# Runs of four up and four down products from place 32 on, a paired softmax, fewer filler products and a later clearing in a windowed attention with a feed-forward layer

## The chip, the cores and the metric

The kernel runs on one core of one Trainium2 chip. A core has five engines that work side by side and meet at semaphores: TensorE (PE, with its weight loads as PEld), VectorE (DVE), ScalarE (ACT), GpSimd (POOL) and SyncE (SP), which issues the DMAs. TensorE writes to PSUM, which has eight banks. The metric is the device time of one execution in microseconds (us).

## The reference

Attention in windows, and behind it a feed-forward layer whose weights are in two projections with a leaky bend between them:

```python
# q, k, v: (4, 8, 768, 64); mem_k, mem_v: (4, 8, 8, 64)
for c in range(nc):                       # chunks of 32 queries
    l_start = max(0, c_start - 16)
    r_end = min(S, c_end + 8)
    k_full = np.concatenate([mem_k, k[:, :, l_start:r_end]], axis=2)
    v_full = np.concatenate([mem_v, v[:, :, l_start:r_end]], axis=2)
    scores = scale * np.matmul(q_c, k_full.transpose(0, 1, 3, 2))
    scores = scores - np.max(scores, axis=-1, keepdims=True)
    a = np.exp(scores)
    a = a / (np.sum(a, axis=-1, keepdims=True) + 1e-09)
    out[:, :, c_start:c_end] = np.matmul(a, v_full)
...
# x: (3072, 512) from the attention; w_in: (512, 2048); w_out: (2048, 512)
h = x @ w_in
g = np.maximum(h, 0.0) + alpha * np.minimum(h, 0.0)
return (g @ w_out).astype(np.float32)
```

The two weights are float64 in memory. The kernel turns them into pairs of numbers (high and low) on the chip.

## The kernel before

**Tiles.** The 3072 tokens are 8 blocks of 384 (`NBLK`, `BT`). A block's attention is four units, one for each pair of heads (`NPAIR`), and leaves four tiles of x, each as a high and a low part (`xh`, `xl`). The 2048 inner columns are 16 tiles (`NF`). For a block and an f, `hidden` makes one *place*: an **up product** (L614: 12 matmuls of 384 columns into one of two PSUM banks, `h_ps`), then the bend (`below` on ACT, L623; `bend` on DVE, L626), the split of its result into `gh` and `gl` (L632, L636), and a **down product** (L644: 9 matmuls of 512 columns, added up in three banks, `o_ps`, over a block's f). There are 128 places. `ORDER` puts (0, f) and (1, f) side by side for the first nine f, so that places 0 to 17 use each weight twice while it is decoded; then blocks 0 and 1 finish, and from place 32 on each block's 16 places follow each other. The first two up products of a block are given out in four pieces of three matmuls, one for each x tile.

**Attention of the first two blocks** (units 0 to 7, `windows`). A unit is loaded as `early` (queries and keys in one DMA, values in another, L424; four buffers, so unit u + 4 waits for unit u). `score_products` (L271) writes one of the two banks `s_ps`; `top` (L439, L441, L443) hides what lies outside and takes the maximum, `less` (L447) subtracts it, `exps` (L451) is on ACT, `total` and `inverse` (L455, L458) give the divisor; GpSimd multiplies (L468, L472); `turn` (L480) transposes on TensorE into `o_ps` banks; ACT copies (L485); `values` (L493) makes the attention's output and `split` (L408, L412) the x parts. In front of each score product and each `turn`, `stir` (L257) issues some bfloat16 matmuls on a constant tile, whose output nobody reads: 8 before the first score product, 2 before each other, 1 before each `turn` (`STIR`).

**Attention of the later blocks.** `attend` gives TensorE a step with the values of one unit (L375) and the scores of the next (L289). The softmax (`scores`: L299 to L320), the weights (L334 to L344) and 14 transposes on DVE (L361) run beside the feed-forward. The transposes write only part of `pt`, and a copy only part of `e2`; the rest is cleared once by `zero` (L517, L520) on GpSimd, emitted after the eighth unit. `BEGIN` and `LATER` give the place at which a unit's scores are due; its weights are due three places later and its values four.

**Weights.** `load_w` loads each f's two tiles of 512 KB (L533); `decode` makes the pairs: `rebias` (ACT, L556), `gather` (L564), `ends` (DVE, L568), `join` (DVE, L572), `high` (ACT, L580), `low` (DVE, L583). The first two f are decoded tile by tile, w_in and w_out apart.

**What sets the order.** Every step is added to `Plan` with an engine, a cost in us, what it reads and writes, and often a due time `rest(place) = (128 - place) x PAIR`, PAIR being 4.7. `send` walks through time by these costs: the engine that can start first takes, of the steps that are ready by then, the one with the most time *behind* it. That is the larger of its own `rest` and of its cost, a hop and what its users have behind them:

```python
behind[n] = max(rest, cost + max((behind[m] + lag[engine] for m in users[n]), default=0.0))
```

Here `lag` is 0.07 (2.3 for a load). The order found is fixed in the program: each engine runs its queue in that order and waits at semaphores. An up product has `rest(place)`, a down product `rest(place + 1.5)`. The bends carry their up product's due time; `high` and `low` have none of their own. In a block's last place `store` copies the three `o_ps` banks with ACT (L691) and sends them out (L695); the next block's first down product needs these banks.

Of the kernel before, what the change touches and what calls it, by code (L numbers as in the profile page):

```python
# [89 lines left out]
STARTS_WIN = (0, 2 * LEFT, NKT - KW)  # L90
# [66 lines left out]
def body(ctx: ExitStack, tc: tile.TileContext, qvw, kw, first, w_in, w_out, alpha, out):  # L157
# [34 lines left out]

    es = [at.tile([P, NJ * 2, KW + 1], F32, name="e", tag=f"e{i}") for i in range(2)]
    for e in es:
        nc.gpsimd.memset(e[:, :, KW:], 1e-9)
    for ew in ews:
# [61 lines left out]

    def score_products(u):
        blk, pr = divmod(u, NPAIR)  # L260
        st = state[u]
        s_ps = ps_s.tile([P, 512], F32, name="s_ps", tag=f"s{u % 2}")
        stir(s_ps, STIR[0] if u == 0 else STIR[1])
        st["s"] = s_ps[:, :2 * NJ * KW].rearrange("p (n k) -> p n k", k=KW)
        t = early[u % NSET]
        q = t[:, :NQ].rearrange("p (c x) -> p c x", c=NT * NJ)
        keys = t[:, NQ:NQ + NT * NKT].rearrange("p (t k) -> p t k", t=NT)
        for n in range(2 * NJ):
            for i in range(2):
                t, j = n // NJ * 2 + i, n % NJ  # L270
                nc.tensor.matmul(  # L271
                    out=st["s"][i * 2 * CH:(i + 1) * 2 * CH, n],
                    lhsT=q[:, t * NJ + j],
                    rhs=keys[:, t, STARTS_WIN[j]:STARTS_WIN[j] + KW],
                    start=True, stop=True,
                )

    def head_products(u):

        st = state[u]  # L280
        st["s"] = [ps_s.tile([P, 512], F32, name="s_ps", tag=f"s{h2}")[:, :NJ * KW].rearrange("p (n k) -> p n k", n=NJ)
                   for h2 in range(2)]
# [20 lines left out]
    def scores(u):  # L303
# [11 lines left out]
        def exps(i):  # L315
            if i == 0:
                st["e"] = at.tile([P, NJ * 2, KW], F32, name="e", tag=f"e{u % 2}")
                st["den"] = sm.tile([P, NJ * 2, 1], F32, name="den", tag=f"den{u % 3}")
            n, h2 = divmod(i, 2)
            nc.scalar.activation(out=st["e"][:, i], in_=st["s"][h2][:, n], func=AF.Exp, scale=SCALE,  # L320
                                 bias=st["mx"][:, n, h2:h2 + 1], accum_out=st["den"][:, i])
# [4 lines left out]
        for i in range(NJ * 2):  # L326
            step(ACT, 0.54, partial(exps, i), reads=[("s", i % 2), ("mx", u % 3)],
                 writes=[("e", u % 2, i), ("den", u % 3, i)] if i else e_keys(u) + den_keys(u), rest=due(u))

# [89 lines left out]
    def load_first(u):  # L419
# [8 lines left out]
        step(SP, 0.78, partial(load, NQ + NT * NKT, NQ + NT * NKT + NV), writes=[("fv", u % NSET)], rest=due(u))  # L428

    def windows(u):  # L430

        st = state[u]
        sk, tks, ak = ("s", u % 2), [("o", 0), ("o", 1)], ("o", 2) if u % 2 else "a"
        ek = [("ew", u % NPT)]

        def top():
            s = st["s"]
            if u // NPAIR % 2 == 0:
                nc.vector.memset(s[0:2 * CH, 0, 0:LEFT], NEG)  # L439
            else:  # L440
                nc.vector.memset(s[2 * CH:4 * CH, 2 * NJ - 1, KW - NM - RIGHT:KW - NM], NEG)  # L441
            st["mx"] = sm.tile([P, NJ * 2, 1], F32, name="mx", tag=f"mx{u % 3}")
            nc.vector.tensor_reduce(out=st["mx"], in_=s, axis=AX.X, op=ALU.max)  # L443

        def less():
            st["e"] = es[u % 2][:, :, :KW]
            nc.vector.tensor_tensor(out=st["e"], in0=st["s"], in1=st["mx"].broadcast_to([P, NJ * 2, KW]),  # L447
                                    op=ALU.subtract)

        def exps():  # L450
            nc.scalar.activation(out=st["e"], in_=st["e"], func=AF.Exp, scale=SCALE)  # L451

        def total():
            st["den"] = sm.tile([P, NJ * 2, 1], F32, name="den", tag=f"den{u % 3}")
            nc.vector.tensor_reduce(out=st["den"], in_=es[u % 2], axis=AX.X, op=ALU.add)  # L455

        def inverse():
            nc.vector.reciprocal(out=st["den"], in_=st["den"])  # L458

# [39 lines left out]

        step(PE, 1.2, partial(score_products, u), reads=[("qk", u % NSET)], writes=[sk], rest=due(u))  # L500
        step(DVE, 0.66, top, writes=[sk, ("mx", u % 3)])
        step(DVE, 0.55, less, reads=[sk, ("mx", u % 3)], writes=e_keys(u))
        step(ACT, 0.52, exps, writes=e_keys(u))
        step(DVE, 0.56, total, reads=e_keys(u), writes=den_keys(u))
        step(DVE, 0.19, inverse, writes=den_keys(u))
        step(POOL, 0.62, partial(scale, 0), reads=den_keys(u) + e_keys(u), writes=ek)
        step(POOL, 0.5, partial(scale, 1), reads=den_keys(u) + e_keys(u), writes=ek)
        step(PE, 0.90, turn, reads=ek + ["eye"], writes=tks, rest=due(u, 1))
        for t in range(2):
# [37 lines left out]
    def decode_part(k, parts):  # L547
# [39 lines left out]
        if n == 1:  # L587
            step(*((ACT, 1.37) if k[1] else (DVE, 0.72)), partial(gather, [nc.scalar.copy if k[1] else nc.vector.tensor_copy]),
                 writes=r)
        elif f in GATHER_ACT:  # L590
            step(DVE, 0.72, partial(gather, [nc.vector.tensor_copy, None]), writes=r[:1])
            step(ACT, 1.37, partial(gather, [None, nc.scalar.copy]), writes=r[1:])
        else:
# [5 lines left out]
             writes=[("w", i, f, 1) for i in parts])  # L599

    def hidden(blk, f, first_f, last_f):

        first = blk * NPAIR
        joint = blk == 1 and f < NJOINT
        place = PLACE[blk, f]
        hk, sd, gh, gl = (x + str(place % 2) for x in ("h", "sd", "gh", "gl"))
        h = {}

        def up(ks):
            if ks[0] == 0:  # L610
                h["ps"] = ps_h.tile([P, 512], F32, name="h_ps", tag=hk)
            for k in ks:
# [16 lines left out]
        def high():  # L629
            h["gh"] = gp.tile([P, BT], F32R, name="gh", tag=gh)  # L630
            copy = nc.scalar.copy if place < HIGH_ACT else nc.vector.tensor_copy
            copy(out=h["gh"], in_=h["g"])  # L632

        def low():
            h["gl"] = gp.tile([P, BT], F32R, name="gl", tag=gl)
            nc.vector.tensor_tensor(out=h["gl"], in0=h["g"], in1=h["gh"].bitcast(F32), op=ALU.subtract)  # L636

        def down(o_ps):
            if f == first_f:
                banks = [(ps_o, f"o{i}") for i in range(NTT)] if not joint else [(ps_s, "s0"), (ps_s, "s1"), (ps_a, "a")]  # L640
                o_ps.extend(pool.tile([P, DM], F32, name="o_ps", tag=tag) for pool, tag in banks)
            for tt in range(NTT):
# [10 lines left out]
        def add_up():  # L653
            for ks in [[k] for k in range(NK)] if f < 2 else [list(range(NK))]:
                step(PE, 0.521 * len(ks), partial(up, ks),
                     reads=[("w", 0, f, 0), ("w", 0, f, 1)] + [(x, x_slot + k) for k in ks for x in ("xh", "xl")],
                     writes=[hk], rest=rest(place))

        def add_bend():
            step(ACT, 0.5, below, reads=[hk], writes=[sd], rest=rest(place))  # L660
            step(DVE, 0.62, bend, reads=["rise", hk], writes=[sd], rest=rest(place))
            step(*((ACT, 0.51) if place < HIGH_ACT else (DVE, 0.35)), high, reads=[sd], writes=[gh])
# [43 lines left out]
    def unit_begins(u):  # L706
        if u < NWIN:
            windows(u)
        else:
            scores(u)  # L710
# [113 lines left out]
```

## Time and profile before

| | us |
|---|---|
| median of 3 runs | 613.23 |
| lowest, highest | 612.78, 613.33 |
| the profiled execution, by its device time | 612.68 |
| its span, from the first to the last instruction | 610.9 |

The page gives the busy time of each engine and its share of the span, then the chain of work that ended last, followed back from the end. PE and PEld are one engine, so their times overlap. A matmul's own duration holds its way through the array; what a product costs is seen from the starts of the pieces in the chain. The rows by stretches of time give, after the stretch and its length, the busy time of PE, PEld, DVE, ACT and POOL, each with its count of instructions, then the granted TensorE clock, the share of DMA and GB/s. The first stretch of interest ends at about 33 us: until then the first eight units' attention, the loads and the first decoding run at once. Places 0 to 31 follow, until 171 us, then the blocks 2 to 7.

### The profile page before, as it was taken

To read this page: it belongs to the slowest core of one execution; us is meant where nothing else is said; L and a number is where in the kernel's file an instruction comes from. 1 tells how busy PE (TensorE), PEld (TensorE's weight loads), DVE (VectorE), ACT (ScalarE), POOL (GpSimd) and SP (SyncE) were. 2 spreads that over 40 slices of the span, in tenths; PEclk is the share of its full clock that TensorE was granted. 3 is DMA by queue.
4 is the path that set the end of the run, shared out by engine and by line. 5 is a ranking of instruction groups with operands and counts; after the bars stand their busy time and mean duration, and the time that the engine had idled before them with its cause. 6 is when DMAs were issued, how large, how long until landed. Compare 5 with 4: busy or idle time off the path is not lost.

```text
span 610.9 us, 11593 instructions
## 1 busy us (share of the span) xinstructions
PE 605.0 (99%) x4622; PEld 532.9 (87%) x4622; DVE 404.5 (66%) x1012; ACT 215.6 (35%) x596; POOL 34.6 (6%) x61
## 2 busy tenths in 40 slices
PE   8999999999999999999999999999999999999997
PEld 5789999889898888989889889888889888989986
DVE  5888999886777656666666666666666656633332
ACT  3788787634223222322223122322123222121111
POOL 3500000000000000000000000000000000000000
PEclk9999999999999999999999999999999999999999
DMA  8999400114121111201113101221002100010001
GB/s 340 352 408 410 164 0 1 33 32 150 25 96 49 50 50 49 99 3 50 49 50 101 42 9 49 84 67 50 20 30 101 50 18 19 0 54 1 0 1 52
DMA packets 20934, 48.99 MB, mean 80 GB/s; under 512 B 2448, under 2 KB 5520, under 8 KB 20880
## 3 DMA queue, kind: packets, MB, share of 16 engines
q1 hardware_dynamic: 20880, 48.25, 22.3%
q8 instruction: 36, 0.59, 0.4%
q14 instruction: 18, 0.15, 0.1%
HBM read 41.95 MB, written 6.29 MB: 79 GB/s over the span
## 4 chain that ended last, share of the span: by engine, by line
PE 97%; DVE 1%; DMA 1%; issue 0%; ACT 0%; SPq 0%; ACTq 0%
PE h_ps L614 44%; PE o_ps L644 44%; PE a_ps L375 3%; PE s_ps L289 3%; PE s_ps L257 1%; PE s_ps L271 1%; DMA w_t<-w_in 1%; PE a_ps L493 1%; PE o_ps L480 0%; DVE w_t L568 0%; PE o_ps L257 0%; DVE mx L443 0%; DVE e L447 0%; DVE w_t L564 0%; DVE xl L412 0%
## 5 line engine op out<-in xcount | busy, mean ns | idle before, releaser
L614 PE MATMUL h_ps<-xh,w 128*128 128x384 f32 x1024 | 261.6, 336 | 0.0
L644 PE MATMUL o_ps<-w,gh 128*128 128x512 f32 x768 | 240.7, 395 | 0.0
L614 PEld LDWEIGHTS h_ps<-xh,w 128*128 128x128 f32 x1024 | 185.7, 188 | 4.2
L614 PE MATMUL h_ps<-xl,w 128*128 128x384 f32 x512 | 174.6, 341 | 0.1
L644 PEld LDWEIGHTS o_ps<-w,gh 128*128 128x128 f32 x768 | 144.0, 188 | 27.8
L644 PE MATMUL o_ps<-w,gl 128*128 128x512 f32 x384 | 150.1, 391 | 0.0
L623 ACT ACTIVATE g<-h_ps 128x384 f32<-128x384 f32 x128 | 63.4, 496 | 245.2 <-PE h_ps L614 236.0
L626 DVE SCALAR_TENSOR_TENSOR g<-g,rise,h_ps 128x384 f32<-128x384 f32 x128 | 78.3, 612 | 94.4 <-ACT g L623 93.3
L361 DVE STREAM_TRANSPOSE pt<-e 32x192 f32<-32x192 f32 (+1 forms) x336 | 99.3, 300 | 11.1 <-POOL e L340 5.9
L614 PEld LDWEIGHTS h_ps<-xl,w 128*128 128x128 f32 x512 | 96.2, 188 | 6.5 <-DVE xl L412 0.3
L644 PEld LDWEIGHTS o_ps<-w,gl 128*128 128x128 f32 x384 | 72.1, 188 | 12.5
L636 DVE TENSOR_TENSOR gl<-g,gh 128x384 fp32r<-128x384 f32 x128 | 71.1, 557 | 4.6 <-ACT gh L632 1.4
L632 DVE CAST gh<-g 128x384 fp32r<-128x384 f32 x104 | 37.2, 360 | 54.2 <-PE o_ps L644 52.4
L320 ACT ACTIVATE e<-s_ps,mx 128x64 f32<-128x64 f32 x144 | 43.3, 320 | 39.7 <-DVE mx L313 39.7
L340 POOL TENSOR_TENSOR e<-e,den 128x384 f32<-128x384 f32 x24 | 20.1, 839 | 467.1 <-DVE den L337 457.4
L408 ACT CAST xh<-a_ps 128x384 fp32r<-128x384 f32 x32 | 15.4, 480 | 55.4 <-PE a_ps L375 53.6
L320 ACT ACTIVATION_READ_ACCUMULATOR e<-s_ps,mx 128x1 f32 x144 | 30.5, 212 | 0.0
L375 PEld LDWEIGHTS a_ps<-pt,v_t 128*64 128x64 f32 x384 | 16.6, 136 | 8.5 <-issue 8.5
L375 PE MATMUL a_ps<-pt,v_t 128*64 128x96 f32 x384 | 21.1, 252 | 0.0
L583 DVE TENSOR_TENSOR w<-a,w 128x1024 fp32r<-128x1024 f32 (+1 forms) x18 | 20.3, 1135 | 0.0
L572 DVE SCALAR_TENSOR_TENSOR a<-a,w_t 128x1024 int32<-128x1024 int32 (+1 forms) x18 | 19.8, 1102 | 0.2
L556 ACT ACTIVATE a<-w_t 128x1024 f32<-128x1024 f32 (+1 forms) x18 | 18.8, 1048 | 2.9 <-DMA w_t<-w_in 1.6
(52 smaller groups left out, 278.3 us busy)
## 6 DMA issues: line engine op xcount, KB each, us to landing
w_t<-w_in SPq DMA_DIRECT2D x16, 512.0 KB, 10.2
w_t<-w_out SPq DMA_DIRECT2D x16, 512.0 KB, 10.2
qk<-kw SPq DMA_DIRECT2D x24, 272.0 KB, 3.7
v_t<-qvw SPq DMA_DIRECT2D x24, 256.0 KB, 2.8
out<-o_t SPq DMA_DIRECT2D x24, 256.0 KB, 2.1
early<-first SPq DMA_DIRECT2D x8, 656.0 KB, 5.9
qk<-qvw SPq DMA_DIRECT2D x24, 192.0 KB, 3.6
early<-first SPq DMA_DIRECT2D x8, 256.0 KB, 5.9
```

What stands on the lines that cost most here:

```text
L320: nc.scalar.activation(out=st["e"][:, i], in_=st["s"][h2][:, n], func=AF.Exp, scale=SCALE, bias=st["mx"][:, n, h2:h2 + 1], accum_out=st["d ...
L340: nc.gpsimd.tensor_tensor(out=st["e"], in0=st["e"], in1=st["den"].broadcast_to([P, NJ * 2, KW]), op=ALU.mult)
L361: nc.vector.transpose(out=pts[u % NPT][quad * CH:(quad + 1) * CH, j, t0:t0 + n1 - n0].rearrange("p t h q -> p (t h) q"), in_=(st["e"], zer ...
L375: nc.tensor.matmul(out=st["a"][h2 * D:(h2 + 1) * D, t * TQ:(t + 1) * TQ], lhsT=st["v"][:, t, h2, :], rhs=pts[u % NPT][:, :, t, h2, :], sta ...
L572: nc.vector.scalar_tensor_tensor(out=d["a"], in0=d["a"], scalar=3, in1=d["t"][:, :, :, 1], op0=ALU.logical_shift_left, op1=ALU.bitwise_or)
L583: nc.vector.tensor_tensor(out=d["w"][:, :, 1], in0=d["a"].bitcast(F32), in1=d["w"][:, :, 0].bitcast(F32), op=ALU.subtract)
L614: nc.tensor.matmul(out=h["ps"][:, :BT], lhsT=ws[f, 0][:, wk, k * P:(k + 1) * P], rhs=xs[first + k][xk], start=(k == 0 and n == 0), stop=(k ...
L623: nc.scalar.activation(out=h["g"], in_=h["ps"][:, :BT], func=AF.Relu, scale=-1.0)
L626: nc.vector.scalar_tensor_tensor(out=h["g"], in0=h["g"], scalar=rise[:, f:f + 1], in1=h["ps"][:, :BT], op0=ALU.mult, op1=ALU.add)
L632: copy(out=h["gh"], in_=h["g"])
L636: nc.vector.tensor_tensor(out=h["gl"], in0=h["g"], in1=h["gh"].bitcast(F32), op=ALU.subtract)
L644: nc.tensor.matmul(out=o_ps[tt], lhsT=h[gk][:, tt * P:(tt + 1) * P], rhs=ws[f, 1][:, wk], start=(f == first_f and i == 0), stop=(f == last ...
```

## The change

Five things are changed.

- **Order.** From place 32 (`FIRST_RUN`) on, places are taken in groups of four (`RUN`). `up_at` and `down_at` replace the places in the due times. There are four `gh`/`gl` pairs instead of two (`NSUM`); the two new ones lie in the decode's tiles (`room`), and their first writers wait for the decode's last use of these.
- **Paired softmax.** Among the first eight units, 2 and 3, 4 and 5, and 6 and 7 go through `softmax` two at a time (`GROUPS`): one `tensor_reduce`, one subtraction, one exponential, one sum and one reciprocal for both. Units 4 and 5 have their scores in the two `h_ps` banks, which are now one tile, as the two `s_ps` banks are.
- **Fewer unread products.** `STIR` goes from (8, 2, 1) to (8, 0, 0), with the planned costs of the score product and of `turn` lowered to 0.76 and 0.68.
- **Later clearing.** `zero` is added when f reaches 9 in block 0, place 18, and waits for the decode of f = 8.
- **Due places.** `BEGIN` moves one place later, `LATER` two places earlier. The gather of the first w_out tile goes from ACT to DVE.

```diff
-BEGIN = {2: (3, 5, 7, 9)}
-LATER = (-1, 3, 7, 11)
-STIR = (8, 2, 1)
+BEGIN = {2: (4, 6, 8, 10)}
+NSUM = 4
+RUN, FIRST_RUN = 4, 32
+LATER = (-3, 1, 5, 9)
+STIR = (8, 0, 0)
+GROUPS = ((0,), (1,), (2, 3), (4, 5), (6, 7))
...
+    h_banks = ps_h.tile([P, 2, 512], F32, name="h_ps")
+    s_banks = ps_s.tile([P, 2, 512], F32, name="s_ps")
...
+    def softmax(us):
+        u0, n = us[0], len(us)
...
+        two, keys = (h_banks, ["h0", "h1"]) if u0 == 4 and n == 2 else (s_banks, [("s", 0), ("s", 1)])
+        here, ring = slice(u0 % 2, u0 % 2 + n), u0 // 2 % 2
...
+        view = two[:, here, :2 * NJ * KW].rearrange("p b (n k) -> p b n k", k=KW)
...
+            nc.vector.tensor_reduce(out=d["mx"], in_=view, axis=AX.X, op=ALU.max)
...
+            nc.vector.tensor_tensor(out=e[..., :KW], in0=view, in1=d["mx"].broadcast_to([P, n, NJ * 2, KW]),
+                                    op=ALU.subtract)
...
+            nc.scalar.activation(out=e[..., :KW], in_=e[..., :KW], func=AF.Exp, scale=SCALE)
...
+            nc.vector.tensor_reduce(out=d["den"], in_=e, axis=AX.X, op=ALU.add)
...
+            nc.vector.reciprocal(out=d["den"], in_=d["den"])
...
-            step(*((ACT, 1.37) if k[1] else (DVE, 0.72)), partial(gather, [nc.scalar.copy if k[1] else nc.vector.tensor_copy]),
-                 writes=r)
+            copy = nc.scalar.copy if k == (1, 1) else nc.vector.tensor_copy
+            step(*((ACT, 1.37) if k == (1, 1) else (DVE, 0.72)), partial(gather, [copy]), writes=r)
...
+    def room(name, tag):
+        n = int(tag[2:])
+        if n < 2:
+            return gp.tile([P, BT], F32R, name=name, tag=tag)
+        if name not in spare:
+            spare[name] = dec.tile([P, 2, DM], F32R, name=name, tag=f"a{len(spare)}")
+        return spare[name][:, n - 2, :BT]
...
+        up_at, down_at = place, place + 1.5
+        if place >= FIRST_RUN:
+            n = place % RUN
+            up_at = place - n + 0.58 + 0.5 * n
+            down_at = place - n + 0.5 * (RUN + n + 1) if n < RUN - 1 else place - n + 1.5 * RUN
...
-                     writes=[hk], rest=rest(place))
+                     writes=[hk], rest=rest(up_at))
...
-                 rest=rest(place + 1.5))
+                 rest=rest(down_at))
...
-    step(POOL, 3.0, zero, writes=["e2"] + [("pt", i, j) for i in range(NPT) for j in range(len(TURNS))] + [("ew", i) for i in range(NPT)])
...
+        if (blk, f) == (0, NJOINT):
+            step(POOL, 3.0, zero, reads=[("w", 1, f - 1, 1)], writes=["e2"] + [("ew", i) for i in range(NPT)]
+                 + [("pt", i, j) for i in range(NPT) for j in range(len(TURNS))])
```

More of the change, by code (lines that the diff above doesn't have):

```diff
@@ L191, in body @@
                             channel_multiplier=1)
-    es = [at.tile([P, NJ * 2, KW + 1], F32, name="e", tag=f"e{i}") for i in range(2)]
+    es = [at.tile([P, 2, NJ * 2, KW + 1], F32, name="e", tag=f"ee{i}") for i in range(2)]
     for e in es:
-        nc.gpsimd.memset(e[:, :, KW:], 1e-9)
+        nc.gpsimd.memset(e[..., KW:], 1e-9)
     for ew in ews:
@@ L257, in stir, with score_products @@
             nc.tensor.matmul(out=t, lhsT=busy[:, :P], rhs=busy, start=True, stop=True)
[L259 to L260 removed]
+    def score_products(u, bank):
         st = state[u]
[L262 to L264 removed]
+        stir(bank, STIR[0] if u == 0 else STIR[1])
+        s = bank[:, :2 * NJ * KW].rearrange("p (n k) -> p n k", k=KW)
         t = early[u % NSET]
@@ L280, in head_products @@
         st = state[u]
-        st["s"] = [ps_s.tile([P, 512], F32, name="s_ps", tag=f"s{h2}")[:, :NJ * KW].rearrange("p (n k) -> p n k", n=NJ)
-                   for h2 in range(2)]
+        st["s"] = [s_banks[:, h2, :NJ * KW].rearrange("p (n k) -> p n k", n=NJ) for h2 in range(2)]
         for n in range(NJ):
@@ L327, in scores @@
             step(ACT, 0.54, partial(exps, i), reads=[("s", i % 2), ("mx", u % 3)],
-                 writes=[("e", u % 2, i), ("den", u % 3, i)] if i else e_keys(u) + den_keys(u), rest=due(u))
+                 writes=[("e", u % 2, i), ("den", u % 3, i)] if i
+                 else e_keys(u) + den_keys(u) + [("ee", u % 2, j) for j in range(2)], rest=due(u))
     def weights(u):
@@ L428, in load_first, with top, less, exps @@
         step(SP, 0.78, partial(load, NQ + NT * NKT, NQ + NT * NKT + NV), writes=[("fv", u % NSET)], rest=due(u))
+    def softmax(us):
+        u0, n = us[0], len(us)
+        d = {}
+        two, keys = (h_banks, ["h0", "h1"]) if u0 == 4 and n == 2 else (s_banks, [("s", 0), ("s", 1)])
+        here, ring = slice(u0 % 2, u0 % 2 + n), u0 // 2 % 2
+        keys, e = keys[here], es[ring][:, here]
+        mk = [("mw", u0)]
+        dk, ek = [[(x, ring, i) for i in range(2)][here] for x in ("dw", "ee")]
+        view = two[:, here, :2 * NJ * KW].rearrange("p b (n k) -> p b n k", k=KW)
+        def top():
+            for i, u in enumerate(us):
+                if u // NPAIR % 2 == 0:
+                    nc.vector.memset(view[0:2 * CH, i, 0, 0:LEFT], NEG)
+                else:
+                    nc.vector.memset(view[2 * CH:4 * CH, i, 2 * NJ - 1, KW - NM - RIGHT:KW - NM], NEG)
+            d["mx"] = sm.tile([P, n, NJ * 2, 1], F32, name="mx", tag=f"mw{n}")
+            nc.vector.tensor_reduce(out=d["mx"], in_=view, axis=AX.X, op=ALU.max)
+        def less():
+            nc.vector.tensor_tensor(out=e[..., :KW], in0=view, in1=d["mx"].broadcast_to([P, n, NJ * 2, KW]),
+                                    op=ALU.subtract)
+        def exps():
+            nc.scalar.activation(out=e[..., :KW], in_=e[..., :KW], func=AF.Exp, scale=SCALE)
+        def total():
+            d["den"] = sm.tile([P, n, NJ * 2, 1], F32, name="den", tag=f"dw{n}{ring}")
+            nc.vector.tensor_reduce(out=d["den"], in_=e, axis=AX.X, op=ALU.add)
+        def inverse():
+            nc.vector.reciprocal(out=d["den"], in_=d["den"])
+            for i, u in enumerate(us):
+                state[u]["e"], state[u]["den"] = e[:, i, :, :KW], d["den"][:, i]
+        for u, key in zip(us, keys):
+            step(PE, 0.76, partial(score_products, u, two[:, u % 2]), reads=[("qk", u % NSET)], writes=[key], rest=due(u))
+        step(DVE, 0.13 + 0.04 + 0.4 * n + 0.065 * n, top, writes=keys + mk)
+        step(DVE, 0.14 + 0.4 * n, less, reads=keys + mk, writes=ek)
+        step(ACT, 0.2 + 0.32 * n, exps, writes=ek)
+        step(DVE, 0.15 + 0.41 * n, total, reads=ek, writes=dk)
+        step(DVE, 0.18 + 0.01 * n, inverse, writes=dk)
@@ L445, in less @@
[L445 to L455, printed above, removed]
@@ L498, in values @@
                     )
[L500 to L508, printed above, removed]
+        step(POOL, 0.62, partial(scale, 0), reads=dk + eu, writes=ek)
+        step(POOL, 0.5, partial(scale, 1), reads=dk + eu, writes=ek)
+        step(PE, 0.68, turn, reads=ek + ["eye"], writes=tks, rest=due(u, 1))
         for t in range(2):
@@ L605, in hidden @@
         place = PLACE[blk, f]
-        hk, sd, gh, gl = (x + str(place % 2) for x in ("h", "sd", "gh", "gl"))
+        hk, sd, gh, gl = (x + str(place % n)
+                          for x, n in (("h", 2), ("sd", 2), ("gh", NSUM), ("gl", NSUM)))
+        if place < FIRST_RUN:
+            gh, gl = f"gh{place % 2}", f"gl{place % 2}"
+        new = [("a", 0), ("a", 1)] if gh in ("gh2", "gh3") and place < FIRST_RUN + NSUM else []
+        up_at, down_at = place, place + 1.5
[3 more added lines that the diff above has]
+            down_at = place - n + 0.5 * (RUN + n + 1) if n < RUN - 1 else place - n + 1.5 * RUN
         h = {}
@@ L610, in up @@
             if ks[0] == 0:
-                h["ps"] = ps_h.tile([P, 512], F32, name="h_ps", tag=hk)
+                h["ps"] = h_banks[:, place % 2]
             for k in ks:
@@ L639, in down @@
             if f == first_f:
-                banks = [(ps_o, f"o{i}") for i in range(NTT)] if not joint else [(ps_s, "s0"), (ps_s, "s1"), (ps_a, "a")]
-                o_ps.extend(pool.tile([P, DM], F32, name="o_ps", tag=tag) for pool, tag in banks)
+                if joint:
+                    o_ps.extend([s_banks[:, 0], s_banks[:, 1], ps_a.tile([P, DM], F32, name="o_ps", tag="a")])
+                else:
+                    o_ps.extend(ps_o.tile([P, DM], F32, name="o_ps", tag=f"o{i}") for i in range(NTT))
             for tt in range(NTT):
@@ L656, in add_up @@
                      reads=[("w", 0, f, 0), ("w", 0, f, 1)] + [(x, x_slot + k) for k in ks for x in ("xh", "xl")],
-                     writes=[hk], rest=rest(place))
+                     writes=[hk], rest=rest(up_at))
         def add_bend():
-            step(ACT, 0.5, below, reads=[hk], writes=[sd], rest=rest(place))
-            step(DVE, 0.62, bend, reads=["rise", hk], writes=[sd], rest=rest(place))
-            step(*((ACT, 0.51) if place < HIGH_ACT else (DVE, 0.35)), high, reads=[sd], writes=[gh])
+            step(ACT, 0.5, below, reads=[hk], writes=[sd], rest=rest(up_at))
+            step(DVE, 0.62, bend, reads=["rise", hk], writes=[sd], rest=rest(up_at))
+            step(*((ACT, 0.51) if place < HIGH_ACT else (DVE, 0.35)), high, reads=[sd], writes=[gh] + new)
             step(DVE, 0.56, low, reads=[sd, gh], writes=[gl])
@@ L707, in unit_begins @@
         if u < NWIN:
+            for us in GROUPS:
+                if us[0] == u:
+                    softmax(us)
             windows(u)
```

23 lines of the change are left out of this document (7 added, 16 removed).

## The prediction

> **What bounds the kernel now.** I read the page first (busy time, then the chain of work that ended last), then the busy time by stretches, then the chain and the timeline in two places: the start and a steady piece.
>
> ```profile
> span 610.9 us, 11593 instructions
> ...
> PE 605.0 (99%) x4622; PEld 532.9 (87%) x4622; DVE 404.5 (66%) x1012; ACT 215.6 (35%) x596; POOL 34.6 (6%) x61
> ...
> PE 97%; DVE 1%; DMA 1%; issue 0%; ACT 0%; SPq 0%; ACTq 0%
> ```
>
> ```profile
> 5.00:24.00 19.00, 18.36 (x288) 13.20 (x288) 14.91 (x39) 9.10 (x20) 7.39 (x18) 1.00 0.99 376
> 24.00:33.50 9.50, 9.40 (x104) 7.55 (x102) 8.59 (x20) 8.45 (x19) 4.92 (x9) 1.00 1.00 375
> 33.50:45.00 11.50, 11.46 (x70) 10.31 (x71) 9.65 (x15) 9.43 (x15) 0.00 (x0) 1.00 1.02 411
> ...
> 300.00:611.00 311.00, 307.24 (x2219) 273.35 (x2217) 178.92 (x483) 74.14 (x253) 10.19 (x13) 1.00 0.12 39
> ```
>
> TensorE is the bound: 97% of the chain is PE. In the rows by stretches (time, length, then busy PE, PEld, DVE, ACT, POOL, clock, DMA share, GB/s) PE is busy throughout from 33.5 us, and in the last one its 3.8 us of idleness are the final copies and stores. So after 33.5 us a gain must make PE's own work shorter. Before that PE is busy too, but not all with work that anyone reads, and DMA (0.99, 1.00) and DVE (8.59 of 9.5 us) are close behind. These two stages are priced apart.
>
> **The steady stage: runs of four.** The chain in order of time (start us, us, what), pieces from four places:
>
> ```profile
> 51.02 4.12 PE o_ps L644 x18
> 55.14 4.18 PE h_ps L614 x24
> ...
> 82.34 2.10 PE h_ps L614 x12
> 84.45 2.08 PE o_ps L644 x9
> ...
> 171.34 1.06 PE h_ps L614 x6
> 172.40 2.08 PE o_ps L644 x9
> 174.48 5.22 PE h_ps L614 x30
> ...
> 601.08 6.18 PE o_ps L644 x27
> ```
>
> An up product is 12 matmuls, a down product 9. An up behind a down takes 2.10 us (82.34), a down behind an up 2.08 (84.45). But two downs in a row take 4.12, so the second costs 2.04: 0.04 less. Two ups in a row take 4.18, the second 2.08: 0.02 less; the 30 at 174.48 agree, as the 18 matmuls behind the first 12 take 3.12, and so do the 27 of the last downs, whose 6.18 holds PE's last drain. Each change of kind costs about 0.04 us into downs and 0.02 into ups, and the later product had its own waits as well, so it is the change of kind, not the start of a step.
>
> Place 32 begins at 171 us. From there to the end the timeline has 89 downs directly behind an up and 71 ups directly behind a down (first 172.40, last 601.08; the other runs start behind attention products).
>
> Which order does the new priority give? The planner takes, of the ready steps, the one with the most time behind it. An up carries its own cost, that of `below` and two hops, 2.72 us by the planner's numbers in the kernel, above its due time; that is 0.58 of PAIR. With `up_at` = group + 0.58 + 0.5n the ups rank at 0, 0.5, 1, 1.5; the downs at 2.5, 3, 3.5, and the fourth at 6, which is 2.0 in the next group. So a group reads: up 0, attention, up 1, up 2, up 3, the fourth down of the group before, then three downs. That is one change each way per group: 24 in 96 places. At the five block ends between places 48 and 112 the next block's first down must wait for the copies out of its banks, and I expect the planner to slip one up between: 29 each way. The attention products stand inside the ups now; their number stays, and their entry and exit are taken as equally dear, so they drop out. The sum: (89-29) x 0.04 + (71-29) x 0.02 = 2.4 + 0.8 = **3.2 us saved**.
>
> What hid the bends and may not now: `h_ps` has two banks, so up 2 waits for the bend of up 0, and up 3 for that of up 1. Before, a down stood between. At block starts three ups already run together:
>
> ```profile
> 385.62 0.36 DVE L310 TENSOR_REDUCE mx<-s_ps 128x3 f32<-128x192 f32 x1
> 385.90 0.55 DVE L412 TENSOR_TENSOR xl<-a_ps,xh 128x384 fp32r<-128x384 f32 x1
> ...
> 389.33 0.34 ACT L320 ACTIVATE e<-s_ps,mx 128x64 f32<-128x64 f32 x1
> 389.53 0.23 ACT L320 ACTIVATION_READ_ACCUMULATOR e<-s_ps,mx 128x1 f32 x1
> ...
> 395.92 0.33 PE L614 MATMUL h_ps<-xl,w 128*128 128x384 f32 x1
> ...
> 396.12 0.49 ACT L623 ACTIVATE g<-h_ps 128x384 f32<-128x384 f32 x1 [1.17 <-PE h_ps L614]
> ...
> 396.64 0.61 DVE L626 SCALAR_TENSOR_TENSOR g<-g,rise,h_ps 128x384 f32<-128x384 f32 x1 [0.43 <-ACT g L623]
> ...
> 398.00 0.33 PE L614 MATMUL h_ps<-xl,w 128*128 128x384 f32 x1
> ```
>
> The middle up starts at 395.92, `below` of the first at 396.12, its bend ends at 397.25, and the third up starts at 398.00: 0.75 us to spare. ACT's exponentials (0.43 us from one's start to its readout's end) and one DVE piece (0.55) can each stand in front, for the attention now falls into the up run: at worst 0.98 against 0.75, so 0.23 us per such up. The bounds are 0 and 24 x 2 x 0.23 = 11 us; the row nearest is the block start, where it is nothing, and both delays rarely meet, so I take 0.4 us. If ups 2 and 3 stall, PE idles, since the fourth down ranks behind up 3. `high` and `low` are covered by the later ups. The two further `gh`/`gl` pairs are needed for this: four downs wait with their inputs in store; they lie in the decode's tiles, free long before place 34.
>
> **The start.** The chain there, and five rows of its timeline:
>
> ```profile
> 1.45 3.60 PE s_ps L257 x8
> 5.05 1.48 PE s_ps L271 x24
> ...
> 12.44 0.60 PE s_ps L257 x2
> 13.04 0.85 PE s_ps L271 x24
> 13.89 0.32 PE o_ps L257
> 14.21 0.66 PE o_ps L480 x6
> 14.87 0.81 PE a_ps L493 x16
> 15.68 0.54 PE s_ps L257 x2
> ...
> 22.07 0.33 SPq L424
> 22.40 0.04 issue
> 22.44 5.25 DMA w_t<-w_in
> ```
>
> ```profile
> 6.72 0.56 DVE L443 TENSOR_REDUCE mx<-s_ps 128x6 f32<-128x384 f32 x1
> ...
> 21.91 0.59 DVE L568 TENSOR_SCALAR w_t<-w_t 128x512 int32<-128x512 int32 x1
> ...
> 28.48 0.89 DVE L564 COPY w_t<-w_t 128x512 int16<-128x512 int16 x1 [0.79 <-ACT a L556]
> ...
> 29.67 1.04 DVE L568 TENSOR_SCALAR w_t<-w_t 128x512 int32<-128x512 int32 x1
> ...
> 29.69 0.74 POOL L520 MEMSET pt<- 128x768 f32 x1
> ```
>
> Per unit PE spends 0.54 + 0.85 + 0.32 + 0.66 + 0.81 = 3.18 us, and 0.86 of it are `stir` products that nothing reads. The change keeps the first eight and drops 7 x 0.54 + 8 x 0.32 = 6.3 us. That is the upper bound. The lower is nothing, where DVE or DMA ends last anyway. What do they allow?
>
> DVE: the same reduction is 0.36 us for 192 columns (L310) and 0.56 for 384 (L443), so 0.16 is fixed. A pair saves that three times and about as much for its reciprocal, 0.64; three pairs, 1.9 us. The second weight's gather moves from ACT to DVE: +0.9 (L564). The later clearing takes GpSimd's memsets out from beside L568, which took 1.04 beside one and 0.59 without: -0.45. Net -1.5 us on an engine that was busy for 8.59 of 9.5. Clearing at place 18 stands where PE is covered by its own products, and costs nothing unless the first transposes, six places later, wait for it.
>
> DMA: `SP` stood at 22.07 until the third unit's values were done, and the weight that starts the late chain was issued only then. Three units earlier by 0.86 each, that is 2.6 us. Against it, a pair's first unit waits for its second, and more loads then meet on full queues. Between 1.5 and 2.6 I take **2.2 us**.
>
> Starting attention two places earlier in each block changes no count of products and PE has no wait there now: 0.
>
> **The sum.** Against the profiled run: 612.68 us (span 610.9 and 1.8 around it) - 3.2 + 0.4 - 2.2 = 607.7. The median of the runs shown is 613.23, 0.55 above that execution; I say **608.0**.
>
> **Rivals.**
> - *Slower: TensorE's clock falls back.* The first `stir` products took 3.60 / 8 = 0.45 us, later ones 0.27 to 0.30; the first score product took 1.48 us, later ones 0.85. So PE began slow and became fast under unbroken work, and the change removes the filler. About 7 x 0.85 + 8 x (0.66 + 0.81) = 17.7 us of work follow. Slow throughout, they cost 0.74 as much again, 13.1 us, less the 6.3 of filler: 612.7 - 2.8 + 6.8 = 616.7. It decides from (6.3 + 2.8) / 0.74 = 12 us of that work run slow. Against it: 2.32 us of real work per unit remain, and DVE's 14.91 us in the first stretch are under 2.5 per unit done there, so I estimate no idle stretch of PE over some 1.5 us. The Trainium skill ("TensorE: Matmul & The Clock Gate", Part 1 on HAM oscillation) says that the rate halves after an idle window of about 3.4 us, which would spare this kernel; its Part 4 on PE-mode transpose says that transposes do not count as busy, which speaks against the change, since 0.66 of the 2.32 us are transposes. No run here shows either. 6 in 100.
> - *Slower: the bends lose their cover.* At 0.23 us in both late ups, 11 us: 612.7 - 5.4 + 11 = 618.3. It decides from 5.4 / 24 = 0.22 us per group. Against it: the block start. 7 in 100.
> - *The order isn't four and four*: the fourth down falls between ups 2 and 3, two changes each way; half the gain, 609.3. 8 in 100.
> - *The start gains nothing*, since DVE and DMA set it: 609.9. 18 in 100.
> - *A change of kind costs nothing*, and the 0.04 and 0.02 stay with the steps: 610.9. The same page (Part 2, Back-to-back issue gap) makes the spacing depend on the columns alone. The rows at 51.02 and 55.14 differ from that. 3 in 100.
>
> My forecast keeps 58. The range: at the low end no bend stalls and the start gains 5 (most of the filler): 612.7 - 3.2 - 5 = 604.5; at the high end the start gains nothing and the bends take 1.5 us: 611.0. I say 604.5 to 611.0; the two slower rivals lie outside, with a part of the others' spread. One measurement of this kernel can tell some 0.2%, 1.2 us, from no change. Faster by more: 84 in 100; within it: 6; slower: 10, nearly all of it the first two rivals.
>
> **What would show it.** In the chain: pieces of 48 ups (or 12 and 36 around attention) and 36 downs after place 32, a down of 2.04 us. If up 3 starts more than 0.1 us behind up 2's last matmul, waiting for DVE, the bends have lost cover. At the start: one score product at 0.85 us, not 1.48, all the way; the first weight's chain ahead of 27.7; the unbroken PE stretch begins near 31 instead of 33.5. I am wrong if the two-bank tile is guarded as a whole (then every up waits for the bend before it), or if the saving at the start is spent again on decoding, whose DVE load in 33.5 to 45 was 9.65 of 11.5 us.

## The result and the profile after

| | us |
|---|---|
| median before, 5 runs of the comparison | 613.25 |
| median after, 5 runs | 670.0 (669.68 to 671.01) |
| ratio | 1.0929, 95% interval 1.0915 to 1.0944 |
| span of the profiled execution, before and after | 610.9 and 667.9 |

The kernel became 9.3% slower; the forecast was 608.0 us, with a range of 604.5 to 611.0. The page of after, and its busy time by stretches (time, length, then PE, PEld, DVE, ACT and POOL busy with their counts, the granted clock, DMA share, GB/s):

```profile
span 667.9 us, 11420 instructions
...
PE 611.5 (92%) x4600; PEld 531.2 (80%) x4600; DVE 395.7 (59%) x1001; ACT 209.7 (31%) x592; POOL 34.2 (5%) x61
...
PE 88%; DVE 6%; ACT 3%; issue 1%; POOL 0%; DVEq 0%; POOLq 0%; ACTq 0%
```

```profile
5.00:24.00 19.00, 15.84 (x265) 13.59 (x264) 12.29 (x28) 7.65 (x16) 4.45 (x12) 0.82 0.89 330
24.00:33.50 9.50, 8.18 (x88) 6.83 (x90) 9.00 (x16) 7.36 (x16) 6.73 (x14) 1.00 0.97 336
...
300.00:668.00 368.00, 332.85 (x2378) 290.35 (x2377) 182.26 (x508) 75.62 (x270) 10.80 (x13) 1.00 0.11 35
```

Before, PE was 97% of the chain and had no idle time after 33.5 us except the end. Now it is 88%, and DVE and ACT hold 9%: in the last stretch PE is idle for 35 us. Who it waits for stands in the view of waits (engine, line, releaser: us in total, times, longest us):

```profile
PEld h_ps L656 <- DVE g L668: 55.1, 41, 2.1
...
PE h_ps L656 <- DVE g L668: 41.7, 37, 1.9
```

L656 is the up product, L665 `below`, L668 the bend, L688 the down product; the two lines are the same waits, seen at the weight load and at the matmul, and don't add up. Here is the first group of four of a block in the chain (start us, us, what), from its first up product to the down products and the next group's attention:

```profile
424.42 1.59 PE h_ps L656 x9
426.01 0.81 PE a_ps L381 x16
426.82 0.66 PE s_ps L294 x45
427.48 1.28 PE h_ps L656 x6
428.76 0.02 issue
428.78 0.50 ACT g L665
429.28 0.04 issue
429.32 0.81 PE h_ps L656 x3
...
430.22 0.62 DVE g L668
430.85 0.04 issue
430.89 3.44 PE h_ps L656 x18
434.32 0.02 issue
434.35 0.50 ACT g L665
434.85 0.03 issue
434.87 0.63 DVE g L668
435.50 0.04 issue
435.54 2.37 PE h_ps L656 x12
437.91 6.16 PE o_ps L688 x27
...
446.18 0.81 PE a_ps L381 x16
```

The four ups come in a row, as forecast, but the run is broken. `below` of up 0 starts only at 428.78, at the end of six matmuls, of which the last three are already up 1's first piece, in the other bank. Up 1's second piece waits for this `below`, and its third (430.89) for the bend, though both read the other bank. At 434.32 PE stands until the `below` and the bend that started only then are through: 1.2 us. They belong to up 1, which had ended some 2 us earlier. Up 3, which waits for them, writes up 1's bank and needs them in any case; but `below` had first waited for up 2, which writes the other bank. So ups wait for bends and bends wait for ups in the other bank, each time for what the program has ahead of it. Attention to attention takes 20.2 us (426.01 to 446.18).

The middle groups of a block stop once, before up 3, and take 19.8 us (446.18 to 465.93):

```profile
447.65 4.38 PE h_ps L656 x24
...
452.05 0.50 ACT g L665
...
452.58 0.62 DVE g L668
...
453.25 2.37 PE h_ps L656 x12
455.62 8.20 PE o_ps L688 x36
463.82 2.11 PE h_ps L656 x12
465.93 0.81 PE a_ps L381 x16
```

The start is slower too, in another way. The timeline of PE there:

```profile
7.92 0.92 PE L277 MATMUL s_ps<-early 128*64 128x64 f32 x24 [1.39 <-DVE e L458]
...
9.64 1.22 PE L277 MATMUL s_ps<-early 128*64 128x64 f32 x24 [0.80 <-DVE mx L455]
...
11.51 1.54 PE L277 MATMUL s_ps<-early 128*64 128x64 f32 x24 [0.66 <-DVE e L458]
```

The second unit's scores, in the second `s_ps` bank, wait for the subtraction that reads the first unit's scores out of the first (1.39 us). And from about 10 us the score products take 1.2 and 1.5 us: the clock is at 0.82 in that stretch.

**Theories.** G: a tile that spans two banks is guarded as a whole, so that whoever touches one bank waits for all that precedes it in the other; the loss is the joined tiles'. C, the rival that the prediction had priced at 11 us: the bends have lost their cover, since one up of 2.08 us is too short for what stands between an up and the next but one; the loss is the runs'. Besides, it was open what the missing filler did.

### The profile page after: what moved, and what is told of

It reads as the page before. It is cut to its first block, busy times and chain, and to the rows that moved or that the text cites. A ratio compares the mean times of both kernels' runs of the same rounds, so it can differ in the third digit from the quotient of the medians.

```text
span 667.9 us, 11420 instructions
## 1 busy us (share of the span) xinstructions
PE 611.5 (92%) x4600; PEld 531.2 (80%) x4600; DVE 395.7 (59%) x1001; ACT 209.7 (31%) x592; POOL 34.2 (5%) x61
## 4 chain that ended last, share of the span: by engine, by line
PE 88%; DVE 6%; ACT 3%; issue 1%; POOL 0%; DVEq 0%; POOLq 0%; ACTq 0%
PE h_ps L656 43%; PE o_ps L688 36%; DVE g L668 4%; ACT g L665 3%; PE a_ps L381 3%; PE s_ps L294 2%; PE s_ps L688 2%; PE o_ps L507 1%; PE s_ps L277 1%; PE a_ps L520 1%; PE s_ps L265 1%; DVE gl L678 0%; DVE mx L455 0%; PE h_ps L277 0%; DVE e L458 0%
## 5 line engine op out<-in xcount | busy, mean ns | idle before, releaser
L656 PE MATMUL h_ps<-xh,w 128*128 128x384 f32 x1024 | 261.5, 336 | 0.0
L688 PE MATMUL o_ps<-w,gh 128*128 128x512 f32 x732 | 227.0, 391 | 0.0
L656 PE MATMUL h_ps<-xl,w 128*128 128x384 f32 x512 | 179.2, 350 | 45.3 <-DVE g L668 41.7
L668 DVE SCALAR_TENSOR_TENSOR g<-g,rise,h_ps 128x384 f32<-128x384 f32 x128 | 76.6, 611 | 202.8 <-ACT g L665 175.6
L656 PEld LDWEIGHTS h_ps<-xh,w 128*128 128x128 f32 x1024 | 185.7, 188 | 1.7
L665 ACT ACTIVATE g<-h_ps 128x384 f32<-128x384 f32 x128 | 60.8, 491 | 344.0 <-PE h_ps L656 330.2
L688 PEld LDWEIGHTS o_ps<-w,gh 128*128 128x128 f32 x732 | 137.4, 188 | 27.9
L656 PEld LDWEIGHTS h_ps<-xl,w 128*128 128x128 f32 x512 | 96.0, 188 | 64.3 <-DVE g L668 55.1
L688 PE MATMUL o_ps<-w,gl 128*128 128x512 f32 x366 | 142.9, 390 | 1.6 <-DVE gl L678 1.6
L688 PEld LDWEIGHTS o_ps<-w,gl 128*128 128x128 f32 x366 | 68.7, 188 | 15.5 <-DVE gl L678 2.0
L346 POOL TENSOR_TENSOR e<-e,den 128x384 f32<-128x384 f32 x24 | 20.2, 840 | 502.0 <-DVE den L343 480.6
L735 ACT COPY o_t<-o_ps 128x512 f32<-128x512 f32 x21 | 12.3, 590 | 45.8 <-PE o_ps L688 44.6
```

The costliest lines, as they stand in the source:

```text
L346: nc.gpsimd.tensor_tensor(out=st["e"], in0=st["e"], in1=st["den"].broadcast_to([P, NJ * 2, KW]), op=ALU.mult)
L656: nc.tensor.matmul(out=h["ps"][:, :BT], lhsT=ws[f, 0][:, wk, k * P:(k + 1) * P], rhs=xs[first + k][xk], start=(k == 0 and n == 0), stop=(k ...
L665: nc.scalar.activation(out=h["g"], in_=h["ps"][:, :BT], func=AF.Relu, scale=-1.0)
L668: nc.vector.scalar_tensor_tensor(out=h["g"], in0=h["g"], scalar=rise[:, f:f + 1], in1=h["ps"][:, :BT], op0=ALU.mult, op1=ALU.add)
L688: nc.tensor.matmul(out=o_ps[tt], lhsT=h[gk][:, tt * P:(tt + 1) * P], rhs=ws[f, 1][:, wk], start=(f == first_f and i == 0), stop=(f == last ...
```

## The experiments

Each was timed with the kernel before on the same chip; a ratio is to that kernel, with its 95% interval.

**1. Two tiles for the `h_ps` banks.**

```diff
-    h_banks = ps_h.tile([P, 2, 512], F32, name="h_ps")
+    h_banks = [ps_h.tile([P, 1, 512], F32, name="h_ps", tag=f"h{i}") for i in range(2)]
...
-        two, keys = (h_banks, ["h0", "h1"]) if u0 == 4 and n == 2 else (s_banks, [("s", 0), ("s", 1)])
+        two, keys = s_banks, [("s", 0), ("s", 1)]
...
-                h["ps"] = h_banks[:, place % 2]
+                h["ps"] = h_banks[place % 2][:, 0]
```

> The changed kernel with the two h_ps banks as two tiles instead of one (units 4 and 5 then take the s_ps banks as the other pairs do). Theory G: a two-bank tile is guarded as a whole, so an up waits for the bend of the up just before it, in the other bank. Then the 46 us that are lost from place 36 on go, and the time falls to 614 to 623 us; what stays is the loss up to place 32, and groups last 18.3 us. Rival C: the bends have lost their cover, because one up of 2.08 us is too short for below and bend and what stands before them. Then nothing changes: 660 to 670 us, groups of 20.3 us.

Measured: 611.0 us, ratio 0.9964 (0.995 to 0.9978). That is 59 us less than the changed kernel, 52 of them from place 32 on (its first up starts at 175.3 us here and at 181.8 there). A middle group in the chain of this kernel:

```profile
428.50 2.11 PE h_ps L656 x12
430.61 0.81 PE a_ps L381 x16
431.42 0.66 PE s_ps L294 x45
432.07 6.46 PE h_ps L656 x36
438.54 8.20 PE o_ps L688 x36
446.74 2.11 PE h_ps L656 x12
448.85 0.81 PE a_ps L381 x16
```

Up 0, attention, three ups unbroken, four downs in 8.20 us (2.05 each), and 18.2 us from attention to attention, where the changed kernel's middle group takes 19.8. A block's first group takes 16.7 here (468.59 to 485.31) and 20.2 there. C falls: the order and the cover are those of the changed kernel, and nothing stalls. The time lies even below the range expected.

**2. Two tiles for the `s_ps` banks as well**, and so no pairs, whose view needs both banks in one tile.

```diff
-GROUPS = ((0,), (1,), (2, 3), (4, 5), (6, 7))
+GROUPS = tuple((u,) for u in range(8))
...
-    s_banks = ps_s.tile([P, 2, 512], F32, name="s_ps")
+    s_banks = [ps_s.tile([P, 1, 512], F32, name="s_ps", tag=f"s{i}") for i in range(2)]
```

> As the one before, and the two s_ps banks are two tiles as well; the softmax of all eight first units goes one unit at a time. Theory G: the wait of the second score product for the subtraction of the first (1.4 us of idle PE at 6.5 us) goes too; with the runs of four free of waits the time is 605 to 612 us, below the kernel before. Rival C: 655 us or more. If the start stays slow for lack of the filler products (clock at half for some 7 us), it lies at 611 to 616.

Measured: 607.48 us, ratio 0.9904 (0.9889 to 0.9918). It beats both kernels. The clock stays at 1.00 at the start, with the filler left out.

**3. The runs alone**, in the kernel before: `BEGIN`, `LATER`, the due times `up_at` and `down_at`, `NSUM` and `room` as in the change, nothing else.

> The kernel before with the runs of four alone: due times, four gh/gl pairs and the due places of the later units' attention; tiles, softmax, filler and clearing as before. Theory G and the prediction's term: 3.2 us saved less 0.4 of waits, 609.5 to 611 us. Rival C: 645 to 660 us.

Measured: 609.17 us, ratio 0.9937 (0.9922 to 0.9952). The runs gain 4.2 us. Their chain has the same unbroken pieces:

```profile
430.08 6.44 PE h_ps L638 x36
436.52 8.20 PE o_ps L668 x36
```

**4. The changed kernel without runs.**

```diff
-RUN, FIRST_RUN = 4, 32
+RUN, FIRST_RUN = 4, 128
```

> The changed kernel with up and down products one by one to the end (first run at place 128), all else as changed. Theory G: the guard of the joined tile costs little there, since a down product of 2.08 us stands between an up and the next, in which the bend ends: 616 to 626 us, of which about 10 us arise before place 32. Rival C says the same of the steady part: 614 to 624 us. If the joined tile costs as much without runs (over 640 us), both are wrong.

Measured: 633.28 us, ratio 1.0324 (1.0303 to 1.0345). Above what was expected. The joined tiles, with the other changes, cost some 20 us without any run of four. The waits stand at each block's start above all, where the planner sets two ups in a row. A down between does not save the ups that follow: at 417.88 one waits 0.35 us for `below`, and at 423.55 the next one 1.21 us for a bend, since these had started late. The waits have the same names as in the changed kernel, only fewer:

```profile
PEld h_ps L656 <- DVE g L668: 17.0, 15, 1.8
PE h_ps L656 <- DVE g L668: 11.2, 11, 1.4
```

**5. The joined tile sliced flat.** Experiment 1 with one `h_ps` tile again, as a row of 1024 columns:

```diff
-    h_banks = [ps_h.tile([P, 1, 512], F32, name="h_ps", tag=f"h{i}") for i in range(2)]
+    h_banks = ps_h.tile([P, 1024], F32, name="h_ps")
...
-                h["ps"] = h_banks[place % 2][:, 0]
+                h["ps"] = h_banks[:, place % 2 * 512:place % 2 * 512 + 512]
```

> The first experiment's kernel with the two h_ps banks in one tile again, now as one row of 1024 columns whose halves are sliced, where the change has two rows of 512; units 4 and 5 stay in the s_ps banks. If the guard goes by the tile, the runs stall as in the changed kernel: 655 to 672 us. If it goes by the columns that an instruction touches, and only the three-dimensional slice was read as the whole, the time is that of two tiles, 611 us.

Measured: 673.55 us in one run, 62 us above experiment 1. The guard goes by the tile, not by the shape of the slice. That experiments 1 and 5 differ only in how the same two banks are declared, with units 4 and 5 in the `s_ps` banks in both, also says that no bank is short of anything: the waits are in the program.

**6. The joined `s_ps` tile, one unit at a time** (experiment 1 with the `GROUPS` of experiment 2).

> The first experiment's kernel (two h_ps tiles, the s_ps banks one tile) with the softmax one unit at a time. It lay 3.5 us above the kernel with both split and no pairs. If the joined s_ps tile costs them by its waits, and pairs gain next to nothing, this one lies at 610 to 613 us; if the pairs themselves cost (the first unit waits for the second), at 607 to 608.5.

Measured: 612.79 us, ratio 0.999 (0.9981 to 0.9999). So the joined `s_ps` tile costs 5.3 us against experiment 2, and pairs win 1.8 of it back by the medians (611.0; the intervals of the two ratios lie just apart). The 5.3 us hold a fall of the clock too: all ten executions have a mean of 0.990 to 0.994. Pairs are good, but the tile that they need costs more than they bring.

**7. The filler put back** in the kernel of experiment 2, `STIR` and the two planned costs as before.

```diff
-STIR = (8, 0, 0)
+STIR = (8, 2, 1)
```

> The kernel with both banks split, with the filler products of the kernel before (8, 2, 1) and their planned costs. The part of the prediction that says that dropping the filler gains: 609 to 610 us, 1.5 to 2.2 above the 607.5 without filler. If DVE and DMA set the start: 607 to 608.

Measured: 608.94 us, ratio 0.9924 (0.9911 to 0.9938). Dropping the filler is worth 1.5 us by the medians; the intervals of the two ratios just overlap.

**8. The filler dropped alone**, in the kernel before.

> The kernel before without the later filler products, (8, 0, 0) and the lower planned costs, all else as before. Dropping the filler gains 1.5 to 2.2 us: 611 to 612. If the clock falls back for a 6.8 us window, as in the changed kernel: 614 to 617.

Measured: 612.69 us, ratio 0.9992 (0.9983 to 1.0001): not told apart from no change. The runs spread from 612.09 to 614.78; in the profiled one, of 614.78, the clock fell in a stretch that begins near 33 us:

```profile
24.00:33.50 9.50, 7.55 (x81) 6.08 (x83) 7.94 (x19) 8.01 (x18) 4.29 (x9) 0.98 1.01 377
33.50:45.00 11.50, 11.50 (x77) 10.71 (x74) 8.49 (x14) 9.06 (x14) 0.00 (x0) 0.87 1.02 409
```

**9. The joined tiles alone**, in the kernel before: its `h_ps` tiles become halves of one tile, its `s_ps` tiles halves of another.

```diff
+    h_banks = ps_h.tile([P, 2, 512], F32, name="h_ps")
+    s_banks = ps_s.tile([P, 2, 512], F32, name="s_ps")
...
-                h["ps"] = ps_h.tile([P, 512], F32, name="h_ps", tag=hk)
+                h["ps"] = h_banks[:, place % 2]
...
-        s_ps = ps_s.tile([P, 512], F32, name="s_ps", tag=f"s{u % 2}")
+        s_ps = s_banks[:, u % 2]
```

> The kernel before with the two h_ps banks joined in one tile and the two s_ps banks in another, and nothing else changed. The guard by tile alone: each place where the planner sets two ups in a row, or a score product beside another unit's softmax, waits. From the changed kernel without runs, 20 us above the kernel before, of which some 2 are its start: 625 to 640 us. If the joined tiles cost only in runs of four: 613 to 618 us.

Measured: 642.15 us, ratio 1.0464 (1.0443 to 1.0485). Nothing but the declarations is changed, and 28.6 us are lost, a little above the range. Half of it arises before place 32, whose first up starts at 185.4 us here and at 171.2 in the kernel before.

**10. The clearing tied to late data**, in the kernel of experiment 2.

```diff
-        nc.gpsimd.memset(zeroed["e2"], 0.0)
+        x = ws[NJOINT - 1, 1].bitcast(F32).rearrange("p a b -> p (a b)")
+
+        def clear(t, n):
+            nc.gpsimd.tensor_tensor(out=t, in0=x[:, :n], in1=x[:, :n], op=ALU.subtract)
+
+        clear(zeroed["e2"].rearrange("p n k -> p (n k)"), NJ * 2 * KW)
...
-            nc.gpsimd.memset(pts[i], 0.0)
+            clear(pts[i].rearrange("p j t h q -> p (j t h q)"), NJ * NT * 2 * CH)
```

> The kernel with both banks split and no pairs, with the clearing tied to the data of the ninth weight: GpSimd subtracts a decoded weight from itself (768 and 384 columns) where it wrote zeros, so that it can't start before that weight is there, near 100 us. In the changed kernel the clearing still ran near 30 us, since the plan's order binds no other engine. The prediction's term for it: DVE's shift beside it falls from 1.04 to 0.6 us, and the time by 0 to 0.5 us, 607.0 to 607.5. If the shift was slow for another reason (GpSimd's products): no change, 607.5.

Measured: 606.93 us, ratio 0.989 (0.9876 to 0.9905), the lowest of all, though not told apart from experiment 2. First a row of the changed kernel's GpSimd, then one of experiment 2's DVE and one of this kernel's, the shift in question:

```profile
29.80 0.42 POOL L538 MEMSET e<- 128x384 f32 x1
```

```profile
29.00 1.04 DVE L589 TENSOR_SCALAR w_t<-w_t 128x512 int32<-128x512 int32 x1
```

```profile
29.08 0.40 DVE L594 TENSOR_SCALAR w_t<-w_t 128x512 int32<-128x512 int32 x1
78.00 0.84 POOL L541 TENSOR_TENSOR e<-w 128x384 f32<-128x384 f32 x1 [48.89 <-ACT w L606]
```

In the changed kernel the clearing is not later: it runs at 29.80 us, where in the kernel before it ran at 29.19. The planner's step waits for a weight, but that only moves its place in GpSimd's own queue, where nothing stood in between; no semaphore binds it. Tied to data it runs at 78 us, and DVE's shift takes 0.40 instead of 1.04 us.

**11. The filler put back in experiment 1**, where the clock fell.

> The first experiment's kernel (two h_ps tiles, the s_ps banks one tile, pairs) with the filler of the kernel before. There the clock was at half from 10.3 to 17.1 us. If that cost more than the filler takes, the filler keeps the clock up and the time falls from 611.0 to 608.5 to 610. If the half clock was covered by waits for the softmax, it stays at 611 to 612.5.

Measured: 612.66 us, ratio 0.9997 (0.9984 to 1.001), against 611.0 without filler. The clock of the profiled execution stays at 1.00 at the start, and yet it is no faster. Experiment 1 says the same by itself: two of its five executions kept a mean clock of 1.0, at 610.09 and 612.1 us, and the three that lost it took 610.85 to 611.73. So the half clock at the start did not decide the time. That waits for the softmax covered it is not shown: in the chain of the changed kernel PE's slow products stand without a break from 11.51 to 18.13 us. Nor is the filler a safeguard: four of this experiment's ten executions have a mean clock of 0.993 to 0.997.

## Why the prediction was wrong

- **The step that failed** is in the part on the steady stage: "`h_ps` has two banks, so up 2 waits for the bend of up 0, and up 3 for that of up 1." It took the guard from the banks, and the sum put these waits at 0.4 us. Once the two banks are one tile, `below` of up 1 waits for up 2 in the other bank, and up 3 for the bend that this delays; in a block's first group up 1 waits for `below` and bend of up 0 as well. PE's waits before up products came to 41.5 us from 182 us on, 38.0 of them for the bend and 3.5 for `below`. I named the guard as something that would make me wrong, with neither a chance nor a price, and not quite as it is: not every up waits for the bend before it, in a middle group one of four does. A price could be had, by estimate: about 1.2 us for `below` and bend at each wait, which is 29 us at one in each of 24 groups and over 80 at three. Experiments 1, 5 and 9 show the cause: two tiles for one take 59 us away with runs, and two pairs of banks joined cost 28.6 us without.
- **The same step at the start.** Joining the `s_ps` banks I cost at nothing. It cost 5.3 us with single units and 3.5 net of the pairs' gain (experiments 6 and 2).
- **The rival that gave the right sign** named the right waiter, PE for DVE's bend, and its sign came (up 3 starts 1.2 us behind up 2's last matmul), but its reason was wrong. The cover is there: with two tiles the bends end in time, and no wait is left in the runs (experiments 1 to 3).
- **The runs' own term was right, and too small.** Its 3.2 less 0.4 us came to 4.2 in the time (experiment 3). Summing the gaps between the starts of matmuls over the base of each kind (0.173 us for an up's, 0.227 for a down's) in the traces of the kernel before and of experiment 3, from place 32 on, gives 9.7 us of surplus in the one and 5.9 in the other, so 3.8 us. There are 25 changes into downs and 24 into ups, not 29 each way, as the planner slips no lone up between at block ends. A change into ups costs 0.026 us and one into downs 0.041, where two decimals gave 0.02 and 0.04. And with two tiles the 0.4 us for waits are nothing. The order was forecast rightly, and that a change of kind costs nothing is refuted by the gain.
- **The start's term, 2.2 us**, was near where the tiles allow it: experiment 2 lies 1.7 us below experiment 3, and the filler's part is 1.5 by the medians of experiments 7 and 2, though alone in the kernel before it wasn't told apart from nothing (experiment 8). The signs came in experiment 2: the load that starts the late chain ends at 27.23 us instead of 27.69, and PE's unbroken stretch begins at 31.68 instead of 33.54. But its makeup was partly wrong. The pairs' gain can't be had without the joined tile. The clearing's 0.45 us were credited to a move that did not take place; made to happen, it takes 0.64 us off one shift, more than forecast, since the row of 0.59 us that I took for undisturbed stood beside a GpSimd product (21.60 to 22.22 us). Its gain in time is not told apart from nothing.
- **The clock.** The rival's event took place, in four of the five executions of the changed kernel and in three of the five of experiment 1: 0.82 over 19 us is 6.8 us at half. It did not decide the time (experiments 1 and 11). In the profile of experiment 2 PE had more to do in its first stretches, and the clock stayed up. For the rule of the Trainium skill that I cited ("TensorE: Matmul & The Clock Gate", Part 1 on HAM oscillation) the rows differ: the longest idle stretch of PE in the changed kernel between 6.5 us and the fall near 10 was 1.39 us, not 3.4.

```profile
6.66:10.07 3.41, 1.35 (x38) 1.21 (x40) 2.23 (x6) 0.53 (x1) 0.00 (x0) 1.00 1.02 422
10.07:16.90 6.83, 6.17 (x77) 5.42 (x72) 3.58 (x9) 2.34 (x5) 2.25 (x6) 0.50 0.98 355
```

These are two stretches of the changed kernel: PE busy for 1.35 of 3.41 us, and then the clock at 0.50. In experiment 2 a stretch as long, 0.9 us later, holds 1.99 us of PE's work, and the clock stays up behind it (1.00 from 4.11 us on):

```profile
7.52:10.93 3.41, 1.99 (x50) 1.84 (x51) 2.68 (x7) 0.58 (x2) 1.12 (x3) 1.00 1.00 400
```

In experiment 9, which has the filler and the joined `s_ps` tile, it fell all the same:

```profile
8.15:11.56 3.41, 1.47 (x27) 0.99 (x27) 2.25 (x6) 0.57 (x2) 0.00 (x0) 1.00 1.01 406
11.56:14.97 3.41, 3.41 (x30) 2.26 (x30) 0.85 (x4) 0.48 (x1) 1.12 (x3) 0.50 1.01 376
```

## What to carry to other kernels

In the language of this kernel a tile is the unit of waiting: before joining two buffers to let one instruction read both, look at who writes one half while another engine reads the other, and price that wait for every pair of steps. Put matmuls of one shape in a row, as each change of shape here cost 0.03 to 0.04 us of PE's time, and see that the engine behind has two separate buffers. An order that a planner finds binds only each engine's own queue; what must come later on another engine needs a dependency on data.

## What the runs showed of the hardware that I had not expected

TensorE's clock fell to half without any idle stretch above 1.4 us, after 3.41 us in which it was busy for 40% of the time. The traces hold eight such falls inside a span; before seven of them PE was busy for 1.35 to 1.69 of 3.41 us, and before the eighth (experiment 5) for 2.08, most of it transposes. But 1.67 us in experiment 1 (17.09 to 20.51) and 1.71 in experiment 9 (195.87 to 199.28) brought no fall, and the same program keeps the clock in some executions and loses it in others. So busy time bears on it, with the turn near half of these 3.41 us, and does not settle it alone.

Half speed over 6.8 us at the start cost nothing that could be seen; why is not shown. Where PE is the bound it may be another matter: the one execution of experiment 8 whose profile shows the fall, at 33.14 us, is the slowest of its ten, 614.78 us against at most 613.11.
